# The last output tile of a fused attention and SwiGLU kernel: column parts of 384 and 128 instead of 256, 128 and 128

## The chip, the cores and the metric

The kernel runs on one core of a Trainium2 chip. The metric is device time in microseconds (us), one launch, all inputs and outputs in HBM. TensorE is called PE here (PEld is its weight load), VectorE DVE, ScalarE ACT, SyncE SP. "Span" is the time of the profiled execution that the trace covers; it is about 1.7 us shorter than the device time of the same run.

## The reference

The input `x` is 2048 tokens by 512 features. Two branches read it, and a gate mixes them:

```python
g = sigmoid((x * gate_w).sum(-1, keepdims=True))
a = linear_attention(x, wqkv) @ wo           # 32 heads of 16, phi(t) = (t > 0 ? t + 1 : exp(t)) + 1e-6
b = (silu(x @ w1) * (x @ w3)) @ w2           # F = 1376
return g * a + (1 - g) * b
```

Only the last step matters here. For each of 16 tiles of 128 tokens, the kernel accumulates the attention part and the SwiGLU part in one PSUM tile (15 matmuls per column group: 4 for attention, 1 for the remainder of F, 10 for the 1280 other rows of `w2`), scales it by a value per token and stores it.

## The kernel before

Output tiles 0 to 14 are computed 512 columns wide. The last tile is cut in three column parts, so that its copy out of PSUM and its store can begin while PE still works on the rest:

```python
def emit_out(tb, tt):
    t = tb * TPB + tt
    tsl = slice(tt * P, (tt + 1) * P)
    if t < NT - 1:
        parts = [(0, D, True)]
    else:
        h, q3 = D // 2, 3 * D // 4
        parts = [(0, h, True), (h, q3, False), (q3, D, True)]
    o_out = work.tile([P, D], BF16, tag="o_out", name="o_out")
    lo = 0
    for i, (a, b, store) in enumerate(parts):
        o_ps = psX.tile([P, b - a], FP32, tag=f"XP{2 + (tt + i) % 2}", name="o_ps")
        # ... 15 matmuls into o_ps[:], with columns a:b of W_sb, w2r_sb and w2_sb ...
        if i < 2:
            nc.scalar.activation(out=o_out[:, a:b], in_=o_ps[:], func=ACT.Copy, scale=omg[:, t : t + 1])
        else:
            nc.vector.tensor_scalar(out=o_out[:, a:b], in0=o_ps[:], scalar1=omg[:, t : t + 1],
                                    scalar2=None, op0=ALU.mult)
        if store:
            # ... rows = the tile's rows of the output ...
            nc.sync.dma_start(out=rows[:, lo:b], in_=o_out[:, lo:b])
            lo = b
```

The order of PE's instructions is the program's; the other engines' order is left to a scheduler, and waits come from data dependences.

Of the kernel before, what the change touches and what calls it, by code (L numbers as in the profile page):

```python
# [8 lines left out]
ACT = mybir.ActivationFunctionType  # L9
ALU = mybir.AluOpType  # L10
# [7 lines left out]
def kernel(  # L18
# [12 lines left out]
    nc = tc.nc  # L31
    P = nc.NUM_PARTITIONS

    Bb, S, D = A_x.shape
# [7 lines left out]
    TPB = TB // P  # L42
# [7 lines left out]
    out2d = out.flatten_outer_dims()  # L50
# [31 lines left out]
    out_pairs = out2d[0:TB, :].rearrange("(g p j) d -> g j p d", p=P, j=2)  # L82
# [6 lines left out]
    for tb in range(1, NTB):  # L89
        dq.dma_start(  # L90
            out=xT[:, :, tb * TB : (tb + 1) * TB], in_=x2d[tb * TB : (tb + 1) * TB, :],
# [3 lines left out]
            out=x_sb[:, tb * TPB : (tb + 1) * TPB, :], in_=x_r[:, tb * TPB : (tb + 1) * TPB, :]  # L95
# [4 lines left out]
    with nc.allow_non_contiguous_dma(reason="one gate weight per partition and chunk"):  # L100
        dq.dma_start(
            out=wr_sb[:, :, 2 * FR : NR], in_=gate_w.rearrange("(kc d o) -> d kc o", d=P, o=1)
# [7 lines left out]
    for fcs in (slice(0, FC // 2), slice(FC // 2, FC)):  # L110
# [9 lines left out]
        out=bm, in_=bm, pattern=[[-Dh, HPC], [0, Dh]], compare_op=ALU.is_ge, fill=0.0,  # L120
# [3 lines left out]
        out=bm, in_=bm, pattern=[[Dh, HPC], [0, Dh]], compare_op=ALU.is_ge, fill=0.0,  # L124
# [6 lines left out]
    omg = consts.tile([P, NT], FP32, name="omg")  # L131
# [200 lines left out]
    def emit_out(tb, tt):  # L332
        t = tb * TPB + tt
        tsl = slice(tt * P, (tt + 1) * P)

        if t < NT - 1:
            parts = [(0, D, True)]
        else:
            h, q3 = D // 2, 3 * D // 4
            parts = [(0, h, True), (h, q3, False), (q3, D, True)]  # L340
        o_out = work.tile([P, D], BF16, tag="o_out", name="o_out")
        lo = 0
        for i, (a, b, store) in enumerate(parts):
            o_ps = psX.tile([P, b - a], FP32, tag=f"XP{2 + (tt + i) % 2}", name="o_ps")
            for c in range(KC):
                nc.tensor.matmul(  # L346
                    o_ps[:], lhsT=st[tb, "pqT"][:, c, tsl], rhs=W_sb[:, c, a:b],
                    start=(c == 0), stop=False,
                )
            nc.tensor.matmul(  # L350
                o_ps[:], lhsT=st[tb, "hTr"][:FR, tsl], rhs=w2r_sb[:FR, a:b],
                start=False, stop=False,
            )
            for fc in range(FC):
                nc.tensor.matmul(  # L355
                    o_ps[:], lhsT=st[tb, "hT"][:, fc, tsl], rhs=w2_sb[:, fc, a:b],
                    start=False, stop=(fc == FC - 1),
                )
            if i < 2:
                nc.scalar.activation(  # L360
                    out=o_out[:, a:b], in_=o_ps[:], func=ACT.Copy, scale=omg[:, t : t + 1]
                )
            else:
                nc.vector.tensor_scalar(  # L364
                    out=o_out[:, a:b], in0=o_ps[:], scalar1=omg[:, t : t + 1], scalar2=None,
                    op0=ALU.mult,
                )
            if store:
                rows = out_pairs[t // 2, t % 2] if t < TPB else out2d[t * P : (t + 1) * P, :]
                nc.sync.dma_start(out=rows[:, lo:b], in_=o_out[:, lo:b])  # L370
                lo = b


    k0 = [psM.tile([P, D], FP32, tag="mm", name=f"k0_{t}") for t in range(TPB)]
# [40 lines left out]
    for c in range(KC):  # L415
# [7 lines left out]
        out=kvT_sb[:], in0=kvT_ps[:],  # L423
# [21 lines left out]
    for tb in range(NTB):  # L445
        for fc in range(FC if tb == 0 else 0, FC):
            emit_ffn(tb, fc)
        nx = tb + 1
        for tt in range(TPB):
            if nx < NTB:  # L450
                emit_q(nx, tt, psX, "XP0")
                if tt % 2 == 0:
                    emit_rem(nx, tt // 2, psX, "XP1")
            emit_out(tb, tt)
            if nx < NTB:
                emit_den(nx, tt)
        if nx < NTB:
            emit_norm(nx)
# [30 lines left out]
```

## Time and profile before

| | |
|---|---|
| device time, median of the first 3 runs | 180.38 us (179.85 to 180.57) |
| span of the profiled run | 178.4 us |
| PE busy | 173.6 us, 97% |
| from the first matmul of the last tile to the end of the span | 6.39 us |

The page of the profile, parts 1 and 4: busy time of each engine with its share of the span and its instructions, and the engines' shares of the chain of work that ended last.

```profile
PE 173.6 (97%) x876; PEld 84.5 (47%) x892; DVE 119.8 (67%) x205; ACT 66.6 (37%) x126; POOL 63.2 (35%) x71
...
PE 96%; DMA 2%; issue 1%; DVE 0%; DVEq 0%
```

PE bounds the kernel: until its last matmul, work of another engine counts only where PE waits for it. What the change can touch is the last tile and what follows it, called the tail below. This is the timeline of the tail: start in us, duration in us (for a line of several instructions, from the start of the first to the end of the last), engine, line, operation, shapes, count, and in brackets how long the engine sat idle before it and what released it.

```profile
172.02 0.60 PE L346 MATMUL o_ps<-W_sb,pqT 128*128 128x256 bf16 x4
...
173.66 0.39 PE L346 MATMUL o_ps<-W_sb,pqT 128*128 128x128 bf16 x4
...
173.91 0.47 ACT L360 ACTIVATE o_out<-o_ps,omg 128x256 bf16<-128x256 f32 x1 [1.00 <-PE o_ps L355]
...
174.51 0.39 PE L346 MATMUL o_ps<-W_sb,pqT 128*128 128x128 bf16 x4
...
174.71 0.37 ACT L360 ACTIVATE o_out<-o_ps,omg 128x128 bf16<-128x128 f32 x1 [0.32 <-PE o_ps L355]
...
174.79 0.72 PE L355 MATMUL o_ps<-w_sb,hT 128*128 128x128 bf16 x10
175.61 0.35 DVE L364 TENSOR_SCALAR o_out<-o_ps,omg 128x128 bf16<-128x128 f32 x1 [11.86 <-PE o_ps L355]
```

The reader should see the pitch: 15 matmuls of 256 columns take 173.66 - 172.02 = 1.64 us, 15 of 128 columns 0.85 us. The chain runs from the last matmul through the DVE copy to the last store; ACT's copies have time to spare.

The transfers of the last 2.5 us, in 40 slices of 0.0625 us from 176.0 us on: busy tenths of the 16 DMA engines and GB/s; below, the median time from issue to landing.

```profile
DMA  0030000000000169962000000000000000000000
GB/s 0 0 131 0 0 0 0 0 0 0 0 0 0 33 205 287 279 189 58 0 0 0 0 0 0 0 0 0 0 0 0 0 0 0 0 0 0 0 0 0
...
q14 instruction: 1, 0.01, 0.9%
...
out_dram<-o_out SPq DMA_DIRECT2D x1, 64.0 KB, 1.5
```

The hump from the fourteenth slice on (176.8 us) is the last store. The single slice of 131 GB/s at 176.15 us is one packet of 8192 bytes on queue 14, of the kind "instruction": an engine's instructions being fetched. It was over (0.38 us, at 176.53) before the store's packets began.

### The profile page before, as it was taken

How to read it: one execution, taken by the hardware profiler on the slowest of the kernel's cores; microseconds unless marked ns; L12 is line 12 of the kernel's file. 1: busy time of each engine (PE TensorE's matmuls, PEld its weight loads, DVE VectorE, ACT ScalarE, POOL GpSimd, SP SyncE). 2: the span in 40 equal slices, each digit the busy share in tenths (PEclk: the TensorE clock that was granted, in tenths of full speed). 3: DMA queues.
4: the chain of work that ended last, by engine and by line, in shares of the span. 5: the costliest groups of instructions: out<-in, count | busy, mean ns of one | idle time of the engine just before them, and what ended most of it. 6: DMA issues, size and time to landing. Idle time of an engine off the chain costs nothing.

```text
span 178.4 us, 2473 instructions
## 1 busy us (share of the span) xinstructions
PE 173.6 (97%) x876; PEld 84.5 (47%) x892; DVE 119.8 (67%) x205; ACT 66.6 (37%) x126; POOL 63.2 (35%) x71
## 2 busy tenths in 40 slices
PE   7999999999999999999999999999999999999993
PEld 3544444474444545444454544444545444444463
DVE  0688867998998737498786375878754669776000
ACT  3642323467532333342333333242433323341221
POOL 5187575767363323262003232620032328000000
PEclk9999999999999999999999999999999999999999
DMA  5999989910015010124000111240001022200011
GB/s 164 251 269 264 262 275 371 343 46 21 15 21 98 0 48 29 44 59 88 0 4 7 37 37 37 60 93 2 0 7 64 10 66 62 59 0 0 29 45 49
DMA packets 29085, 14.88 MB, mean 83 GB/s; under 512 B 19632, under 2 KB 28816, under 8 KB 29072
## 3 DMA queue, kind: packets, MB, share of 16 engines
q1 hardware_dynamic: 28800, 14.46, 30.0%
q10 hardware_dynamic: 272, 0.26, 0.5%
q8 instruction: 7, 0.11, 0.3%
q14 instruction: 6, 0.05, 0.1%
HBM read 8.42 MB, written 2.10 MB: 59 GB/s over the span
## 4 chain that ended last, share of the span: by engine, by line
PE 96%; DMA 2%; issue 1%; DVE 0%; DVEq 0%
PE gate_ps L310 19%; PE o_ps L355 19%; PE up_ps L318 19%; PE q_ps L217 8%; PE o_ps L346 8%; PE XP L204 8%; PE k_ps L184 6%; PE r_ps L241 3%; PE o_ps L350 2%; PE k L184 2%; DMA x_sb<-in_A_x_dram 2%; PE xTp L174 1%; PE kvT_ps L418 1%; PE W_ps L440 0%; DVE o_out L364 0%
## 5 line engine op out<-in xcount | busy, mean ns | idle before, releaser
L310 PE MATMUL gate_ps<-xT,w_sb 128*128 128x512 bf16 x157 | 40.9, 379 | 0.2
L318 PE MATMUL up_ps<-xT,w_sb 128*128 128x512 bf16 x156 | 40.7, 379 | 0.2
L225 POOL TENSOR_TENSOR qz<-pq,z_sb 128x512 f32<-128x512 bf16 x16 | 18.5, 1164 | 59.4 <-DVE pq L145 58.4
L323 ACT ACTIVATE th<-gate_ps 128x512 bf16<-128x512 f32 x40 | 23.9, 597 | 37.9 <-PE gate_ps L310 37.5
L355 PE MATMUL o_ps<-w_sb,hT 128*128 128x512 bf16 (+2 forms) x177 | 37.4, 354 | 0.2
L325 DVE SCALAR_TENSOR_TENSOR gs<-th,gate_ps 128x512 bf16<-128x512 bf16 x40 | 27.3, 683 | 5.6 <-ACT th L323 5.3
L328 DVE TENSOR_TENSOR hT<-up_ps,gs 128x512 bf16<-128x512 f32 x40 | 27.6, 691 | 3.7
L142 DVE TENSOR_SCALAR phi_m<-phi_e 128x512 bf16<-128x512 bf16 x32 | 15.7, 490 | 18.9 <-ACT phi_e L140 18.8
L355 PEld LDWEIGHTS <-hT 128*128 128x128 bf16 x180 | 16.8, 97 | 17.9
L318 PEld LDWEIGHTS <-w_sb 128*128 128x128 bf16 x160 | 15.7, 98 | 18.9
L310 PEld LDWEIGHTS <-w_sb 128*128 128x128 bf16 x160 | 15.6, 98 | 18.6
L360 ACT ACTIVATE o_out<-o_ps,omg 128x512 bf16<-128x512 f32 (+2 forms) x17 | 11.2, 656 | 30.4 <-PE o_ps L355 30.4
L290 POOL TENSOR_TENSOR pqn<-pq,rden 128x512 bf16<-128x512 bf16 x16 | 16.6, 1057 | 14.0 <-DVE rden L283 11.7
L194 POOL TENSOR_TENSOR pks<-pks,pk_sb 128x512 f32<-128x512 f32 x15 | 17.3, 1156 | 8.1 <-DVE pk_sb L145 7.5
L228 DVE TENSOR_REDUCE den<-qz 128x32 f32<-128x512 f32 x16 | 11.0, 685 | 8.3 <-POOL qz L225 8.3
L346 PE MATMUL o_ps<-W_sb,pqT 128*128 128x512 bf16 (+2 forms) x71 | 16.5, 355 | 0.0
L217 PE MATMUL q_ps<-wq_sb,xT 128*128 128x512 bf16 x61 | 16.3, 379 | 0.2
L204 PE MATMUL XP<-pk_sb,x_sb 128*128 128x512 bf16 x62 | 16.0, 379 | 0.1
L140 ACT ACTIVATE phi_e<-k_ps 128x512 bf16<-128x512 f32 x12 | 7.2, 598 | 14.4 <-PE k_ps L184 12.2
L140 ACT ACTIVATE phi_e<-q_ps 128x512 bf16<-128x512 f32 x16 | 9.6, 597 | 7.8 <-PE q_ps L217 6.7
L184 PE MATMUL k_ps<-wk_sb,xT 128*128 128x512 bf16 x48 | 12.3, 379 | 0.1
L145 DVE SCALAR_TENSOR_TENSOR pq<-q_ps,phi_m 128x512 bf16<-128x512 f32 x16 | 11.0, 691 | 0.5
(59 smaller groups left out, 120.4 us busy)
## 6 DMA issues: line engine op xcount, KB each, us to landing
w_sb<-in_B_w_dram SPq DMA_DIRECT2D x6, 640.0 KB, 9.4
out_dram<-o_out SPq DMA_DIRECT2D x15, 128.0 KB, 1.7
x_sb<-in_A_x_dram SPq DMA_DIRECT2D x3, 512.0 KB, 4.3
x_sb<-in_A_x_dram SPq DMA_DIRECT2D x2, 256.0 KB, 3.9
wq_sb<-in_A_wqkv_dram SPq DMA_DIRECT2D x1, 512.0 KB, 6.2
wv_sb<-in_A_wqkv_dram SPq DMA_DIRECT2D x1, 512.0 KB, 6.4
wo_sb<-in_A_wo_dram SPq DMA_DIRECT2D x1, 512.0 KB, 10.8
wk_sb<-in_A_wqkv_dram ACTq DMA_DIRECT2D x1, 256.0 KB, 3.9
```

The lines of the kernel that those rows point to most:

```text
L184: nc.tensor.matmul(k_ps[:], lhsT=xT[:, kc, t * P : (t + 1) * P], rhs=wk_sb[:, kc, :], start=(kc == 0), stop=(kc == KC - 1),)
L194: nc.gpsimd.tensor_add(pks[:], pks[:], pk_sb[:, t, :])
L204: nc.tensor.matmul(XP_ps[dc][:], lhsT=x_sb[:, t, dc * P : (dc + 1) * P], rhs=pk_sb[:, t, :], start=(t == 0), stop=(t == NT - 1),)
L217: nc.tensor.matmul(q_ps[:], lhsT=xT[:, kc, ts_tok], rhs=wq_sb[:, kc, :], start=(kc == 0), stop=(kc == KC - 1),)
L225: nc.gpsimd.tensor_tensor(out=qz[:], in0=st[tb, "pq"][:, tt, :], in1=z_sb[:], op=ALU.mult)
L310: nc.tensor.matmul(gate_ps[:], lhsT=w1_sb[:, kc, fsl], rhs=xT[:, kc, tok_sl], start=(kc == 0), stop=(kc == KC - 1),)
L318: nc.tensor.matmul(up_ps[:], lhsT=w3_sb[:, kc, fsl], rhs=xT[:, kc, tok_sl], start=(kc == 0), stop=(kc == KC - 1),)
L323: nc.scalar.activation(out=th[:], in_=gate_ps[:], func=ACT.Tanh, scale=0.5)
L325: nc.vector.scalar_tensor_tensor(out=gs[:], in0=th[:], scalar=1.0, in1=gate_ps[:], op0=ALU.add, op1=ALU.mult)
L328: nc.vector.tensor_tensor(out=st[tb, "hT"][:, fc, :], in0=up_ps[:], in1=gs[:], op=ALU.mult)
L346: nc.tensor.matmul(o_ps[:], lhsT=st[tb, "pqT"][:, c, tsl], rhs=W_sb[:, c, a:b], start=(c == 0), stop=False,)
L355: nc.tensor.matmul(o_ps[:], lhsT=st[tb, "hT"][:, fc, tsl], rhs=w2_sb[:, fc, a:b], start=False, stop=(fc == FC - 1),)
```

## The change

The intent is to do the last tile in two column parts, 384 and 128: one accumulation group of 15 matmuls and weight loads fewer on PE. Copies and stores keep their sizes: ACT copies 256 columns, then 128, out of the 384-wide PSUM tile; DVE copies the last 128; the two stores stay 256 columns each. The first store can start only when all 384 columns are accumulated.

```diff
         if t < NT - 1:
-            parts = [(0, D, True)]
+            parts = [(0, D, [(0, D, True)])]
         else:
             h, q3 = D // 2, 3 * D // 4
-            parts = [(0, h, True), (h, q3, False), (q3, D, True)]
+            parts = [(0, q3, [(0, h, True), (h, q3, False)]), (q3, D, [(q3, D, True)])]
 ...
-        for i, (a, b, store) in enumerate(parts):
+        for i, (a, b, pieces) in enumerate(parts):
 ...  (the matmuls are the same, over columns a:b)
+            for u, v, store in pieces:
+                if i == 0:
+                    nc.scalar.activation(out=o_out[:, u:v], in_=o_ps[:, u - a : v - a], ...)
+                else:
+                    nc.vector.tensor_scalar(out=o_out[:, u:v], in0=o_ps[:, u - a : v - a], ...)
+                if store:
+                    ...
+                    nc.sync.dma_start(out=rows[:, lo:v], in_=o_out[:, lo:v])
+                    lo = v
```

More of the change, by code (lines that the diff above doesn't have):

```diff
@@ L358, in emit_out @@
                 )
-            if i < 2:
-                nc.scalar.activation(
-                    out=o_out[:, a:b], in_=o_ps[:], func=ACT.Copy, scale=omg[:, t : t + 1]
-                )
-            else:
-                nc.vector.tensor_scalar(
-                    out=o_out[:, a:b], in0=o_ps[:], scalar1=omg[:, t : t + 1], scalar2=None,
-                    op0=ALU.mult,
-                )
-            if store:
-                rows = out_pairs[t // 2, t % 2] if t < TPB else out2d[t * P : (t + 1) * P, :]
-                nc.sync.dma_start(out=rows[:, lo:b], in_=o_out[:, lo:b])
-                lo = b
+            for u, v, store in pieces:
+                if i == 0:
+                    nc.scalar.activation(
+                        out=o_out[:, u:v], in_=o_ps[:, u - a : v - a], func=ACT.Copy,
+                        scale=omg[:, t : t + 1],
+                    )
+                else:
+                    nc.vector.tensor_scalar(
+                        out=o_out[:, u:v], in0=o_ps[:, u - a : v - a],
+                        scalar1=omg[:, t : t + 1], scalar2=None, op0=ALU.mult,
+                    )
+                if store:
+                    rows = out_pairs[t // 2, t % 2] if t < TPB else out2d[t * P : (t + 1) * P, :]
+                    nc.sync.dma_start(out=rows[:, lo:v], in_=o_out[:, lo:v])
+                    lo = v
     k0 = [psM.tile([P, D], FP32, tag="mm", name=f"k0_{t}") for t in range(TPB)]
```

## The prediction

> **What bounds the kernel now.** TensorE does: the page gives PE 173.6 us busy of a 178.4 us span, and the chain of work that ended last is 96% PE. After the last matmul only a tail is left. The change touches the last output tile alone, about 172.0 us to the end, so only those 6.4 us count.
>
> **The tail before (the timeline from 172 us).** The 15 matmuls of 256 columns start at 172.02, the first 15 of 128 columns at 173.66, the second 15 at 174.51, and the last matmul starts at 175.29. ACT copies 256 columns at 173.91 (474 ns) and 128 at 174.71 (367 ns); DVE copies the last 128 at 175.61 (351 ns). SP issues the first 256-column store at 174.41 and the second at 176.02 (332 ns each). The second store's packets run from 176.86; SP sees it landed at 177.58, and 0.8 us of closing barrier follow. The chain is: last matmul, DVE copy, second store, barrier. ACT's copies and the first store are off it.
>
> **What the change does, costed.** From start to start a matmul takes 109 ns at 256 columns (1.64 us / 15) and 56 ns at 128 (0.84 us / 15). That is a straight line with about 2.7 ns per matmul that does not depend on the width. The Trainium skill, "TensorE: Matmul & The Clock Gate", section "Wait — 56ns, not 53.3ns?", gives the same: N / 2.4 GHz plus about 2.5 ns. This trace agrees (55.9 and 109.2 ns). Estimate for 384 columns: 163 ns, so 2.44 us where 1.64 + 0.84 = 2.48 us stood. The weight loads (97 ns each) are already hidden at a pitch of 56 ns, so removing 15 of them gives nothing more. Removed from PE: 15 matmuls and 15 loads, worth about 0.04 us.
>
> Moved: the 256-column ACT copy must wait for the 384-column group. Estimate: start about 174.72 instead of 173.91, end about 175.20; the 128-column ACT copy follows directly and ends about 175.55. The first store is issued about 175.22, 0.8 us later than before. The DVE copy starts about 175.57 and ends about 175.92, so ACT has some 0.35 us to spare, SP is free again at about 175.6, and the second store is issued about 175.98. The first store's packets should run about 176.05 to 176.40 (before, 0.83 us from issue to first packet and 0.35 us of packets), just ahead of the second's at about 176.82. The two stores nearly touch but should not overlap.
>
> **On the critical path:** only the 0.04 us of PE. The 0.8 us delay of the first store is absorbed; the margin left is about 0.35 us on ACT and on SP.
>
> **Prediction.** 180.34 us, range 179.95 to 180.75, mostly the scatter between runs (179.85 to 180.57 before). Chances: faster by over 2% 0.01, within 2% 0.98, slower by over 2% 0.01.
>
> **What would show each step.** The timeline: 15 matmuls of 128x384 at about 163 ns from start to start; the last matmul at about 175.25; the DVE copy at about 175.57, still released by PE; both ACT copies back to back, done before DVE's; the first store issued near 175.2, the second near 175.98, landing 1.5 to 1.6 us later. The chain of waits must still end in PE, DVE, store. PE should have 15 matmuls fewer, all else the same count.
>
> **What would make it wrong.** The second store may be slowed by the first, now about 0.75 us ahead of it instead of 1.6 us: a longer issue (early back-to-back issues took 0.41 to 0.46 us instead of 0.33) or a later landing; that would cost 0.1 to 0.3 us. The second ACT copy might end after DVE's. Or the scheduler orders other work differently elsewhere, which nothing in the change asks for.

## The result

The kernel after took 180.41 us (median of 6 runs, 179.77 to 180.72), the kernel before 180.45 us (6 runs, 179.85 to 180.70). The ratio is 1.0001, with a 95% interval of 0.9977 to 1.0025. The interval is about 0.4 us wide on either side: nothing of 0.1 or 0.2 us can be seen in it, and what follows on that scale is read from traces.

The page of the kernel after, the same two parts:

```profile
PE 173.3 (97%) x861; PEld 83.1 (47%) x877; DVE 119.1 (67%) x205; ACT 66.5 (37%) x126; POOL 63.2 (35%) x71
...
PE 94%; DMA 3%; issue 1%; SPq 0%; DVE 0%; DVEq 0%
```

Fifteen matmuls and fifteen weight loads are gone; every other count is the same, and so is the order of the instructions of the other engines. The timeline of the tail:

```profile
172.13 0.81 PE L346 MATMUL o_ps<-W_sb,pqT 128*128 128x384 bf16 x4
...
174.57 0.39 PE L346 MATMUL o_ps<-W_sb,pqT 128*128 128x128 bf16 x4
...
174.82 0.73 ACT L361 ACTIVATE o_out<-o_ps,omg 128x256 bf16<-128x256 f32 x2 [1.80 <-PE o_ps L355]
174.85 0.72 PE L355 MATMUL o_ps<-w_sb,hT 128*128 128x128 bf16 x10
175.67 0.35 DVE L366 TENSOR_SCALAR o_out<-o_ps,omg 128x128 bf16<-128x128 f32 x1 [11.82 <-PE o_ps L355]
```

The 384-wide group takes 174.57 - 172.13 = 2.44 us, as estimated. This execution reached the last tile 0.105 us later than the traced one of before; that is from earlier in the kernel, which the change does not touch (a second trace of the same kernel reached it at 172.03). Read from the first matmul of the last tile, the last matmul starts after 3.227 us instead of 3.270 us. Both ACT copies are done (175.55 us) before DVE's (176.02 us), and DVE's is still released by PE.

The transfers, in slices of 0.0625 us from 176.0 us on:

```profile
DMA  0027985105000015887200000000000000000000
GB/s 0 0 90 221 303 262 140 33 0 131 0 0 0 0 33 180 270 254 222 74 16 0 0 0 0 0 0 0 0 0 0 0 0 0 0 0 0 0 0 0
...
q14 instruction: 1, 0.01, 1.3%
...
out_dram<-o_out SPq DMA_DIRECT2D x1, 64.0 KB, 1.8
```

The first hump is now the first store and the second the last store. They do not overlap, as predicted. But the last store took 1.8 us to land instead of 1.5, and the instruction fetch (the lone 131) has moved from 176.15 to 176.61 us. It took 0.52 us, until 177.13, and so lies across the start of the last store's packets at 176.92 us.

The Trainium skill, "DMA: Bandwidth & Descriptors", section "Why a DMA increments its semaphore by 16 and not by 1", says that each DMA engine that takes part adds one to the semaphore when its share has landed. The trace agrees, and shows these 16 increments one by one. For the last store, counted from its issue:

| | 15th of 16 shares landed | 16th share landed |
|---|---|---|
| before | 1.510 us | 1.544 us |
| after | 1.542 us | 1.779 us |

One share alone is late, by 0.24 us. The tail can be added up without remainder from four pieces: first to last matmul start, last matmul start to the issue of the last store, issue to landing, landing to end.

| us | matmuls | to the issue | to landing | closing barrier | tail |
|---|---|---|---|---|---|
| before | 3.270 | 0.730 | 1.544 | 0.845 | 6.389 |
| after | 3.227 | 0.731 | 1.779 | 0.830 | 6.567 |

So PE gave the predicted 0.043 us, and 0.235 us went to the landing. Whether that is chance, the nearness of the two stores, or the fetch, the experiments had to say.

### The profile page after: what moved, and what is told of

It reads as the page before. It is cut to its first block, busy times and chain, and to the rows that moved or that the text cites. A ratio compares the mean times of both kernels' runs of the same rounds, so it can differ in the third digit from the quotient of the medians. Undisturbed runs are those within 1.5% of the kernel's fastest.

```text
span 178.7 us, 2443 instructions
## 1 busy us (share of the span) xinstructions
PE 173.3 (97%) x861; PEld 83.1 (47%) x877; DVE 119.1 (67%) x205; ACT 66.5 (37%) x126; POOL 63.2 (35%) x71
## 4 chain that ended last, share of the span: by engine, by line
PE 94%; DMA 3%; issue 1%; SPq 0%; DVE 0%; DVEq 0%
PE gate_ps L310 19%; PE o_ps L355 19%; PE up_ps L318 19%; PE q_ps L217 8%; PE o_ps L346 8%; PE XP L204 8%; PE k_ps L184 6%; PE r_ps L241 3%; DMA x_sb<-in_A_x_dram 3%; PE o_ps L350 2%; PE k L184 1%; PE kvT_ps L420 1%; PE W_ps L442 0%; PE xTp L174 0%; SPq L85 0%
## 5 line engine op out<-in xcount | busy, mean ns | idle before, releaser
L323 ACT ACTIVATE th<-gate_ps 128x512 bf16<-128x512 f32 x40 | 23.9, 597 | 37.9 <-PE gate_ps L310 37.5
L142 DVE TENSOR_SCALAR phi_m<-phi_e 128x512 bf16<-128x512 bf16 x32 | 14.9, 465 | 19.5 <-ACT phi_e L140 19.4
L355 PEld LDWEIGHTS <-hT 128*128 128x128 bf16 x170 | 16.2, 98 | 18.5
```

Source lines behind the costliest of these rows:

```text
L323: nc.scalar.activation(out=th[:], in_=gate_ps[:], func=ACT.Tanh, scale=0.5)
L355: nc.tensor.matmul(o_ps[:], lhsT=st[tb, "hT"][:, fc, tsl], rhs=w2_sb[:, fc, a:b], start=False, stop=(fc == FC - 1),)
```

## The experiments

Three theories of the late share: **F**: an instruction fetch that follows ACT's end falls among the last store's packets. **N**: the first store, now 0.77 us ahead of the last instead of 1.61 us, holds it up; the prediction had named this as its main risk. **C**: chance of one execution. Beside it, the size of the gain itself (2.7 to 2.9 ns for each matmul) was tested by enlarging it.

Eleven runs were made, each with 5 rounds. Those of one group shared a chip and the runs of before.

### Group 1: the kernel after again, and the first attempts to part F from N

**after_again** is the kernel after, unchanged.

> The kernel after, unchanged, for a second trace. In the first one the last store landed 1.78 us after its issue (15 of its 16 shares at 1.54 us), before 1.54 us. Theory F (an instruction fetch of 8192 B, which starts about 1.03 us after ACT's last instruction ended, falls among the packets of the last store): again 1.7 to 1.8 us, one share alone late, the fetch starting near 176.6. Rival N (the first store, now 0.77 us ahead of the last instead of 1.61 us, holds it up): again 1.7 to 1.8 us. Rival C (chance of one execution): 1.54 us. Time: within 0.3% of before under each.

Measured: 180.35 us, ratio 1.0011 (0.9989 to 1.0033). The last store landed after 1.660 us, its 15th share after 1.535 us. The fetch ran from 176.50 to 176.95 us, the store's packets from 176.82 us. So it is not C: the late share came again, smaller, and the overlap with the fetch was smaller too (0.13 us after 0.21 us).

**swap_pieces** is the kernel after with the engines of the two pieces exchanged.

```diff
-                if i == 0:
+                if i == 0 and (b == D or u > 0):
```

> The kernel after, with DVE copying the 256-column piece and ACT the 128-column piece of the 384, side by side. ACT then ends at about 175.2 instead of 175.55, so the fetch should start at about 176.25 and be over before the last store's packets at 176.9. The first store stays 0.75 to 0.8 us ahead of the last. Theory F: last store lands 1.54 us after issue, 0.24 us sooner than in the kernel after; Rival N: 1.7 to 1.8 us. The last DVE copy should still start near 175.6, not held up by DVE's first. Time: about 0.05 us (0.03%) under before with F, not to be seen in the timing.

Measured: 180.34 us, ratio 1.0006 (0.9985 to 1.0027). The two stores were issued 0.69 us apart, nearer than in the kernel after, and the last landed after 1.539 us. That speaks against N. But two things went otherwise than expected. The copies did not run side by side: ACT's waited for DVE's, which read the same PSUM tile. And the fetch did not move to 176.25 us; it left the span altogether. Instead ACT's last drain (the instruction DRAIN, which ACT runs a last time in the closing barrier) came late, at 178.14 us, and landing to end took 1.042 us instead of 0.83 to 0.845. ACT had one instruction fewer here, 193 instead of 194 (counted with semaphore and other instructions that the page's 126 leaves out), which pointed to the number of ACT's instructions as a second thing that places the fetch.

**store_late** was to delay the first store alone.

```diff
-            parts = [(0, h, True), (h, q3, False), (q3, D, True)]
+            parts = [(0, h, False), (h, q3, True), (q3, D, True)]
 ...
-                nc.sync.dma_start(out=rows[:, lo:b], in_=o_out[:, lo:b])
-                lo = b
+                hi = D // 2 if i == 1 else b
+                nc.sync.dma_start(out=rows[:, lo:hi], in_=o_out[:, lo:hi])
+                lo = hi
```

> The kernel before, its matmul parts 256, 128, 128 kept, but the first store is issued only after ACT's second copy: the delay of the store alone, without the wider matmuls. First store at about 175.1 instead of 174.41, last store at 176.02 as before, 0.9 us later. ACT ends at 175.07 as before. Theory F: fetch at 176.1 as before, last store lands in 1.54 us, span as before. Rival N: last store lands 1.65 to 1.8 us after issue. Matmuls from first to last of the last tile: 3.27 us as before.

Measured: 180.46 us, ratio 1.0000 (0.9978 to 1.0023). The edit had no effect. SP still issued the first store 26 ns after ACT's first copy, because a wait follows from the data that an instruction reads and not from its place in the program. The stores stayed 1.61 us apart. The run only serves as a second trace of before: 1.539 us to landing, tail 6.371 us.

**act_late** was to delay ACT's end in the kernel before.

```diff
+                if i == 1:
+                    idle = work.tile([P, 448], BF16, tag="idle", name="idle")
+                    nc.scalar.activation(out=idle[:], in_=<448 columns of x_sb>, func=ACT.Copy)
```

> The kernel before, with one useless ACT copy of 448 columns from SBUF to SBUF after its last real one, so that ACT ends at about 175.55 instead of 175.07, as in the kernel after; stores and matmuls untouched. Theory F: the fetch moves to about 176.6 and one share of the last store lands late, 1.7 to 1.8 us after issue. Rival N: stores are 1.6 us apart as before, so it lands in 1.54 us. Time within 0.3% of before.

Measured: 180.27 us, ratio 1.0004 (0.9982 to 1.0025). It missed its aim for the same reason: the added copy depends on nothing late and ran at 3.9 us. ACT ended as in before, and the last store landed after 1.542 us. But ACT had one instruction more, and the fetch had moved 0.95 us earlier, to 175.20 us, among the packets of the *first* store (175.26 us on). That store's 15th share landed after 1.55 us and its 16th after 1.91 us. So a fetch delays one share of whatever store it meets, in the kernel before as well.

### Group 2: F against N on purpose, and the size of the gain

**after_plus1** is the kernel after with one more ACT instruction.

```diff
+        if t == NT - 1:
+            idle = work.tile([P, 16], BF16, tag="idle", name="idle")
+            nc.scalar.activation(out=idle[:], in_=x_sb[:, 0, 0:16], func=ACT.Copy)
```

> The kernel after with one more short ACT instruction (16 columns, long before the end; it can run early). In the run act_late one more ACT instruction moved the end's 8192 B fetch 0.95 us earlier, to 175.2. The two stores stay 0.77 us apart and ACT still ends near 175.5. Theory F (the fetch, not the nearness of the stores, makes one share of the last store late): fetch well before 176.8, last store lands in 1.54 us, tail from the last tile's first matmul to the end of the span about 6.34 us (before 6.37 to 6.39, after 6.45 and 6.57). Rival N (nearness of the stores): 1.66 to 1.78 us as in the two traces of after, tail 6.45 or more.

Measured: 180.16 us, ratio 0.9997 (0.9977 to 1.0018). The transfers, again from 176.0 us on:

```profile
DMA  2698610000001798610000000000000000000000
GB/s 82 197 295 263 181 33 0 0 0 0 0 0 49 221 279 271 189 41 0 0 0 0 0 0 0 0 0 0 0 0 0 0 0 0 0 0 0 0 0 0
...
out_dram<-o_out SPq DMA_DIRECT2D x1, 64.0 KB, 1.5
```

The two humps of the stores stand as near each other as in the kernel after (0.767 us from issue to issue), but the fetch is gone from between them; it ran at 175.69 us. The last store landed after 1.530 us, and the tail was 6.319 us, as F said (6.34). N is refuted.

**act_late2** is the kernel before, with a useless ACT copy that must come last and one ACT copy of the middle given to DVE, so that ACT keeps its 194 instructions.

```diff
+                if i == 1:
+                    idle = work.tile([P, 3, P], BF16, tag="idle", name="idle")
+                    nc.scalar.activation(
+                        out=idle[:], in_=o_out[:, None, a:b].to_broadcast([P, 3, P]), func=ACT.Copy)
 ...
-        if dc % 2 == 0:
+        if dc == 0:
```

> The kernel before, with a useless ACT copy that must follow the last real one (it reads its result, 3 x 128 columns) and one ACT copy in the middle of the kernel given to DVE, so that ACT has as many instructions as before but ends about 0.45 us later, near 175.5. Stores stay 1.61 us apart, matmuls as before (3.27 us). Theory F: the fetch moves to about 176.55 and one share of the last store lands late, 1.65 to 1.8 us; tail 6.5 us or more. Rival N: lands in 1.54 us, tail 6.38 us.

Measured: 180.87 us, ratio 1.0029 (1.0006 to 1.0053). The copy given to DVE may have cost something in the middle (the last tile began at 172.77 us), so only the tail is compared. The stores stayed 1.608 us apart, and the matmuls took 3.270 us as in before. ACT ended later, the fetch came at 177.42 us, the packets of the last store began at 177.60 us, and its last share landed after 1.804 us (the 15th after 1.544); tail 6.648 us. The transfers from 176.0 us on:

```profile
DMA  5996300000000000000000300159862000000000
GB/s 180 279 303 197 74 8 0 0 0 0 0 0 0 0 0 0 0 0 0 0 0 0 131 0 0 49 188 287 262 172 66 25 0 0 0 0 0 0 0 0
...
out_dram<-o_out SPq DMA_DIRECT2D x1, 64.0 KB, 1.8
```

The first hump is the first store; the lone 131, the fetch, stands just before the last store's hump and runs on into it. The late share is thus made in the kernel before as well, by a later end of ACT at the same number of instructions.

**split_all** enlarges what the change removes: the 15 other output tiles are split too.

```diff
+            for u in range(a, b, P) if t < NT - 1 else (a,):
+                v = u + P if t < NT - 1 else b
+                og = o_ps[:, u - a : v - a]
+                # ... the 15 matmuls into og, with columns u:v ...
```

> The kernel before with the 15 other output tiles split too: four groups of 128 columns in one PSUM bank, still one copy and one store each: 675 more matmuls and weight loads, the same columns. If a matmul costs 2.7 to 2.9 ns besides its columns (15 fewer took 43 ns off the last tile) this is 1.8 to 2.0 us slower, ratio 1.010 to 1.011. If removing a narrow matmul freed more than that (a weight load of 97 ns not hidden at a pitch of 56 ns, 41 ns each) it would be some 27 us slower.

Measured: 182.78 us, ratio 1.0149 (1.0124 to 1.0174), about 2.7 us slower, more than the 1.8 to 2.0 expected and far from 27. Where other work follows, an output tile takes 3.366 us from first to last matmul and on to the next group where it took 3.240 us, so 126 ns for 45 more matmuls: 2.8 ns each, as expected, and 15 x 0.126 = 1.9 us in all. The rest is a new wait in the first output tile of the last block. From the waits of PE, 160 to 170 us:

```profile
PE o_ps L358 <- DVE hT L328: 0.6, 1, 0.6
```

Its first group of 128 columns reaches the last chunk of `hT` 14 narrow matmuls after it began, before DVE has written it; a 512-wide group reaches it only after some 3 us. From start to start that matmul came 0.78 us after its predecessor instead of 0.06, so 0.72 us, and 1.89 + 0.72 = 2.6 us. So the price of a matmul is confirmed, and splitting early has a price of its own that the estimate lacked.

**halves** also has 15 matmuls fewer, in parts of 256 and 256.

```diff
-            parts = [(0, q3, [(0, h, True), (h, q3, False)]), (q3, D, [(q3, D, True)])]
+            parts = [(0, h, [(0, h, True)]), (h, D, [(h, q3, False), (q3, D, True)])]
 ...
-                if i == 0:
+                if i == 0 or v == q3:
```

> Last tile in two parts of 256, so also 15 matmuls fewer, but the first store as early as before; the second half is copied by ACT (128 columns) and DVE (128 columns). Last matmul from first: about 3.21 us. If ACT and DVE read the same PSUM tile side by side, both copies start about 0.36 us after the last matmul's start (0.31 with 128 columns) and the tail is 6.38 to 6.45 us. If they are put one after the other, as ACT's copy was after DVE's in swap_pieces, the last store is issued about 0.35 us later and the tail is 6.75 us.

Measured: 180.78 us, ratio 1.0030 (1.0009 to 1.0051). The copies ran one after the other. From its timeline:

```profile
175.57 0.37 ACT L361 ACTIVATE o_out<-o_ps,omg 128x128 bf16<-128x128 f32 x1 [1.12 <-PE o_ps L355]
175.97 0.35 DVE L366 TENSOR_SCALAR o_out<-o_ps,omg 128x128 bf16<-128x128 f32 x1 [12.16 <-DMA out_dram<-o_out]
```

The store named as releaser had landed before; DVE began 33 ns after ACT's copy ended at 175.935 us, as ACT had waited for DVE in swap_pieces. The last store was issued 1.088 us after the last matmul's start instead of 0.73, the 0.35 us expected for this case. The tail was longer still (7.063 instead of 6.75 us), because the later ACT end put the fetch (176.98 to 177.58 us) among the last store's packets (from 177.18 us): landing after 1.962 us, 15th share after 1.549. The shared output buffer alone does not put copies in a row: in swap_pieces ACT's copy and DVE's last one, out of two PSUM tiles into the same `o_out`, overlapped by 0.10 us. That leaves the shared PSUM tile. The changed kernel's choice, two copies by the same engine out of one PSUM tile and the last one from a tile of its own, avoids this wait.

### Group 3: does the count of ACT's instructions place the fetch?

**swap_plus1** and **swap_plus2** are swap_pieces with one and two short ACT instructions added.

```diff
+        if t == NT - 1:
+            idle = work.tile([P, 32], BF16, tag="idle", name="idle")
+            nc.scalar.activation(out=idle[:, 0:16], in_=x_sb[:, 0, 0:16], func=ACT.Copy)
+            nc.scalar.activation(out=idle[:, 16:32], in_=x_sb[:, 0, 0:16], func=ACT.Copy)   # swap_plus2 only
```

> swap_pieces with one short ACT instruction added, so that ACT has as many instructions as before and after. In swap_pieces ACT had one fewer, no fetch fell inside the span, and ACT's last drain came 0.2 us late in the closing barrier (1.04 us from landing to end instead of 0.83 to 0.845). Theory F: the fetch returns to about 1.03 us after ACT's end (175.6), at about 176.6, and one share of the last store lands late (1.65 to 1.8 us), while the barrier is 0.83 us again. If ACT's late drain in swap_pieces had nothing to do with the instruction count, the barrier stays 1.04 us and the store lands in 1.54 us.

Measured: 181.02 us, ratio 1.0026 (1.0005 to 1.0048). With 194 instructions the fetch was back, and the barrier was 0.829 us again. The transfers from 176.0 us on:

```profile
DMA  0000000000048963000000489630000000000000
GB/s 0 0 0 0 0 0 0 0 0 0 8 156 279 303 205 91 8 0 0 0 0 8 139 262 410 205 82 8 0 0 0 16 25 16 8 0 0 0 0 0
...
q14 instruction: 1, 0.01, 1.1%
```

This is the clearest picture of the mechanism. The second hump is the last store; the 410 in it holds the fetch's packet, which began at 177.51 us and took 0.454 us, so until 177.966. The store has 128 packets, and by the trace 120 of them began between 177.37 and 177.69 us. The other eight began from 177.963 us on: the small hump at the end. Eight is a sixteenth of 128, the share of one DMA engine (the trace does not name the engine of a packet). 15 shares landed by 1.541 us and the last after 2.218 us, 0.68 us late.

The Trainium skill, "DMA: Bandwidth & Descriptors", section "Queues, rings and completion order", says that the ring row 14 is the runtime's own, for refill among other things, and that a DMA engine alternates between the rows it has work for at the granularity of a packet. The trace agrees so far: the fetch is on queue 14, and the eight late packets began when the fetch's packet of 8192 bytes was done; in halves, too, the last eight began as it ended (177.58 us). Such a fetch took 0.31 to 0.61 us in these tails, where a store's packet of 512 bytes takes 0.025 us.

> swap_pieces with two short ACT instructions added: one more than before. Theory F: the fetch comes earlier (near 175.7, as in after_plus1), last store lands in 1.54 us, barrier 0.83 us, last DVE copy 0.26 us after the last matmul's start as in swap_pieces (0.316 in before and after): tail about 6.26 us, 0.12 us under before, too small for the timing (ratio 0.9993).

Measured: 180.30 us, ratio 0.9992 (0.9972 to 1.0011). With 195 instructions the fetch came still earlier, at 173.28 us (expected near 175.7), away from both last stores. The expectation had taken the time from after_plus1. By the traces, in all four runs with 195 the fetch began 1.03 to 1.32 us after the last semaphore instruction before ACT's last drain; that instruction ended at 172.25 us here and at 173.88 to 174.64 us in the other three. Landing 1.541 us, barrier 0.845 us, tail 6.285 us: the shortest of all traces, 0.09 to 0.10 us under the three of before and its equivalents.

**pretouch** is after_plus1 with an early write by DVE into the last output buffer.

```diff
+        if t == NT - 1:
+            nc.vector.memset(o_out[:, 3 * D // 4 : 3 * D // 4 + 8], 0.0)
```

> after_plus1, and DVE writes 8 columns of the last output buffer early, so that its last copy need not wait there for the buffer's former users as well as for the last matmul. If those extra waits are the 58 ns by which the last DVE copy started later in before and after than in swap_pieces, it now starts 0.26 us after the last matmul's start, and the tail is about 6.26 us (after_plus1 6.32, before 6.37 to 6.39). If not, 0.316 us and 6.32 us.

Measured: 180.12 us, ratio 0.9982 (0.9965 to 1.0000). The step it was made for held: the last DVE copy began 0.257 us after the last matmul's start instead of 0.316, so the extra waits for the buffer's former users did cost it 59 ns. The tail still was 6.367 us, not 6.26. SP's issue of the last store took 433 ns instead of 332 ns, and all 16 shares came 0.1 us later. The fetch had met the first store there (its 16th share landed 0.21 us after its 15th). Why the issue grew is open: in after_plus1 the fetch met the first store too, with an issue of 332 ns. As the trace shows no shorter tail than before, the ratio is not taken as a gain.

### All tails together

| us | matmuls | to the issue | to landing | barrier | tail | fetch | last store's packets from | stores apart |
|---|---|---|---|---|---|---|---|---|
| before | 3.270 | 0.730 | 1.544 | 0.845 | 6.389 | 176.15 to 176.53 | 176.86 | 1.608 |
| store_late (acts as before) | 3.270 | 0.732 | 1.539 | 0.830 | 6.371 | 175.90 to 176.41 | 176.64 | 1.612 |
| act_late | 3.269 | 0.731 | 1.542 | 0.839 | 6.381 | 175.20 to 175.51 | 176.87 | 1.610 |
| after | 3.227 | 0.731 | **1.779** | 0.830 | 6.567 | 176.61 to 177.13 | 176.92 | 0.767 |
| after_again | 3.227 | 0.732 | **1.660** | 0.829 | 6.448 | 176.50 to 176.95 | 176.82 | 0.767 |
| act_late2 | 3.270 | 0.729 | **1.804** | 0.845 | 6.648 | 177.42 to 177.82 | 177.60 | 1.608 |
| halves | 3.174 | 1.088 | **1.962** | 0.839 | 7.063 | 176.98 to 177.58 | 177.18 | 1.870 |
| swap_plus1 | 3.228 | 0.671 | **2.218** | 0.829 | 6.946 | 177.51 to 177.97 | 177.37 | 0.686 |
| swap_pieces | 3.227 | 0.673 | 1.539 | 1.042 | 6.481 | none before the end | 176.74 | 0.686 |
| after_plus1 | 3.229 | 0.730 | 1.530 | 0.830 | 6.319 | 175.69 to 176.17 | 176.79 | 0.767 |
| swap_plus2 | 3.228 | 0.671 | 1.541 | 0.845 | 6.285 | 173.28 to 173.75 | 176.75 | 0.686 |
| pretouch | 3.229 | 0.672 | 1.637 | 0.829 | 6.367 | 175.58 to 176.12 | 176.74 | 0.711 |

In the five traces where the fetch overlaps the last store's packets, one share lands 0.12 to 0.68 us after the other fifteen. In the seven where it does not, the last share follows within 0.05 us, whether the stores are 0.69 or 1.61 us apart.

The lateness goes with the overlap: 0.13, 0.21, 0.23, 0.41 and 0.45 us of overlap (after_again, after, act_late2, halves, swap_plus1) went with a share 0.12, 0.24, 0.26, 0.41 and 0.68 us late. Each row of the table is one execution. The timing, six runs each, leans the same way: the three kernels with the longest tails (halves, swap_plus1, act_late2) are the only ones of this table whose interval lies above 1 (halves and act_late2 differ in other ways too).

## Why the prediction was right

The prediction gave 180.34 us and "within 2%" with 0.98; measured were 180.41 us and 1.0001. Point by point:

1. **PE bounds the kernel and only the tail can change.** Right. Except for PE, no engine's instructions changed in number or order, and the earlier part differs only by the scatter of executions (the last tile began at 172.02 to 172.13 us in the traces of before and after).
2. **A matmul costs about 2.7 ns besides its columns.** Right. Fifteen fewer took 43 ns off the last tile, 2.9 ns each; 45 more in split_all added 126 ns to a tile, 2.8 ns each. The Trainium skill, "TensorE: Matmul & The Clock Gate", section "Wait — 56ns, not 53.3ns?", has about 2.5 ns. The steps between matmuls of 128 rows agree: about 55.6, 109.0 and 162.4 ns at 128, 256 and 384 columns, so 2.3 to 2.4 ns over the page's N / 2.4 GHz. The rest stands in the two steps that follow the start of each group's 96-row remainder matmul, which take 60 and 58 ns at 128 columns. The weight loads were hidden already, as stated: had each narrow matmul hidden a cost of 41 ns, split_all would have been 27 us slower.
3. **384 columns at 163 ns.** Right: 2.442 us for 15.
4. **The 0.8 us delay of the first store is absorbed.** Right, and the margins too. ACT was done 0.47 us before DVE's copy ended, more than the 0.35 estimated; its second copy began 0.10 us before the first had ended. SP was free again before the last store was due, its issue took 333 ns as before, and the packets of the two stores did not overlap.
5. **The nearness of the stores as the main risk.** It did not happen: in after_plus1 and swap_plus2 the last store landed in 1.53 and 1.54 us with the stores 0.77 and 0.69 us apart.
6. **The last store lands 1.5 to 1.6 us after its issue.** This is the step that failed. It took 1.78 and 1.66 us in the two traces. The cause was not on the list of risks: the prediction followed ACT's copies only as far as the data they release, and ACT had "0.35 us to spare". But ACT's end also places an instruction fetch, and the change moved that end by 0.37 us relative to the first matmul of the last tile, to where the fetch met the last store.

So the total was right, and one term of it was not. The total is a weak test: the range was 0.8 us wide, more than any term that the change touches. The terms differ: by the traces PE's 0.043 us was more than given back, and the tail of the kernel after (6.45 and 6.57 us) was 0.06 to 0.20 us longer than that of before (6.37 to 6.39 us). The timing can't resolve this: both intervals for the kernel after hold 1. The predicted gain was real and on the path that sets the time, but it was smaller than a side effect that the prediction had not looked for.

That the fetch belongs to ACT is inferred, as the trace does not name the engine that a fetch serves. The ground is that it moved with ACT's end at the same number of instructions (act_late2), that it moved when only ACT's number of instructions changed (after_plus1), and that wherever ACT had 194 instructions it began 1.01 to 1.25 us after ACT's last drain before the barrier had ended. The traces hold one more ground. Another fetch of 8192 bytes, which began at 46.3 to 47.0 us in the other traces of the table, began at 37.0 to 37.9 us in the five runs in which an added ACT instruction ran early (at 3.5 to 4.0 us). Together this fits fetches that are started at fixed places in ACT's instruction stream. For the last one, ACT would reach the place before the drain with 195 instructions, at the drain with 194 and inside the barrier with 193; in swap_pieces a fetch began at 179.04 us, after the span. Why ACT's last drain came late in swap_pieces stays open: one instruction more removed the delay, but the drain was over at 178.27 us, before that fetch's packet began.

No version is clearly faster than before by the timing. By the trace, swap_plus2 has the best tail (6.285 us), because it keeps PE's 0.043 us, saves 0.058 us before the last DVE copy and has its fetch out of the way. Its useless instructions only shift the fetch, so any later edit to ACT's work can undo it.

## What to carry to other kernels

Where matmuls run back to back with hidden weight loads, merging column groups saves only the fixed few nanoseconds of each matmul removed (here 15 x 2.9 ns), so cut the last tile by what its copies and stores need and not by the number of matmuls. A delay that is "absorbed" should be followed to everything that it places, fetches of instructions included: when a last store lands late, look whether one of its 16 shares is late alone, and what else was on the DMA engines. Two engines that copy out of one PSUM tile were put one after the other here, so give the last copy a tile of its own.

## What the Trainium skill lacked or had wrong

- "Runtime: NRT & Kernel Launch", section "Instruction fetch mechanics", gives refills in blocks of 16 KiB and calls the cost of crossing a block mostly hidden. Here seven fetches of 16,384 bytes were on queue 8, and six of 8192 bytes on queue 14, the one at the end among them (kernel before). It has nothing on the cost to other transfers, which was 0.12 to 0.68 us on a store of 64 KB.
- "DMA: Bandwidth & Descriptors", section "Queues, rings and completion order", has the alternation between ring rows, but not what one foreign packet costs: in swap_plus1 all eight packets of one engine's share began only as the fetch's packet of 0.454 us ended.
- The section "Instruction fetch mechanics" ties fetches to markers at block boundaries of the instruction stream, which fits, but gives no time from there to the transfer. With 194 ACT instructions the last fetch began 1.01 to 1.25 us after ACT's drain; with 195 earlier (173.28 to 175.69 us); with 193 after the end of the span.
- "TensorE: Matmul & The Clock Gate", section "Wait — 56ns, not 53.3ns?", was close for matmuls of 128 rows (about 2.5 ns there, 2.3 to 2.4 ns here), but a group with one 96-row matmul came to 2.8 to 2.9 ns each, as the two steps after its start are longer (60 and 58 ns instead of 55 to 56 at 128 columns).
